# First-layer products of the experts: 512 moving columns in one product, or in two of 256

## The chip, the core and the metric

The kernel runs on one core of a Trainium2 chip. The metric is the device time of one execution in microseconds. Engines: PE is TensorE (PEld its loads of stationary operands), DVE VectorE, ACT ScalarE, POOL GpSimd, SP the queue that issues most DMAs.

## The reference

A recurrent attention (768 steps; 4 batches, 8 heads, a 40x40 state each) gives 3072 tokens of 320 numbers. A gate chooses two of eight experts for each token, and each expert is a two-layer network of 320 -> 1024 -> 320. Only the second part is touched:

```python
for e in range(E):
    for k in range(2):
        mask = top2[:, k] == e
        h = np.maximum(x[mask] @ w1[e], 0.0)
        out[mask] += top2_w[mask, k, None] * (h @ w2[e])
```

## The kernel before

The attention comes first, for some 600 us, in chunks of 64 steps; beside it the gate is worked out and tokens get slots in the experts' lists. Then the eight experts run one after the other. Each has room for 832 tokens, in two parts of 512 and 320 (`PARTS`).

For one expert, `load1` and `load2` fetch its float32 weights, and `loadx` gathers its tokens by indirect DMAs on POOL. `trans` (L268) turns the tokens round on PE, 128 at a time, into the PSUM tile `pt`. Weights and tokens are then split into a high and a low piece of type float32r (`split1`, `split2`, and the copies in `trans`), so that the products of pieces together keep float32's accuracy. ACT makes the high piece (w2h, L243) and DVE the low one (w2l, L244).

`hidden` is the first layer. For each part and each of eight blocks of 128 hidden units it takes a PSUM tile `ph` of 128x512 float32 (three buffers) and adds up eight products in it (L287): high by high, low by high, high by low, over 320 inputs in three slices. The moving operand is the tokens, so a product of part 0 has 512 moving columns and one of part 1 has 320. ACT then writes the rectified high piece `hh` (L288), and DVE subtracts for the low piece `hl` (L290), which frees the `ph` buffer.

`output` is the second layer: for each 128 tokens a PSUM tile `po` (three buffers) gets 24 products (L309), eight each of hh by w2h, hl by w2h and hh by w2l, all of 320 moving columns. The last 64 tokens go another way (L300, L301), and ACT (yl, L303) and DVE (y, L304) end them; for the others ACT alone writes y (L310). POOL adds y to the result by an indirect DMA (L311).

The order on each engine is set by the tile framework: it runs a timeline of its own over the program as written and places each instruction when it thinks its inputs are there. So first-layer products of an expert, second-layer products of the same one and transposes for the next stand mixed on PE. A product of float32r loads its own stationary operand: in the program it is one instruction, in the trace a load and a product.

Of the kernel before, what the change touches and what calls it, by code (L numbers as in the profile page):

```python
# [39 lines left out]
class Moe:  # L40
# [236 lines left out]
    def hidden(s,W,X,part):  # L277
        nc=s.nc; wh,wl=W; xh,xl,x3,x3l=X
        t0,n=s.parts[part]; t0%=CAP; r=slice(t0,t0+n)
        m=n//128*128; z=n-m  # L280
        hh=s.hp.tile([128,8,n+z],F32R,name=f"hh{part}"); hl=s.hp.tile([128,8,m],F32R,name=f"hl{part}")
        for f in range(8):
            fs=slice(128*f,128*f+128)
            ph=s.ph.tile([128,512],F32,name="ph",bufs=3)
            mm=[(wh[:,0,fs],xh[:,0,r]),(wh[:,1,fs],xh[:,1,r]),(wh[:,2,fs],x3[:,r]),(wl[:,0,fs],xh[:,0,r]),(wl[:,1,fs],xh[:,1,r]),
                (wh[:,0,fs],xl[:,0,r]),(wh[:,1,fs],xl[:,1,r]),(wh[:,2,fs],x3l[:,r])]
            for i,(a,b) in enumerate(mm): nc.tensor.matmul(ph[:,:n],a,b,start=i==0,stop=i==7)  # L287
            nc.scalar.activation(hh[:,f,:n],ph[:,:n],AF.Relu)  # L288
            for o,c in ((hl[:,f],slice(0,m)),(hh[:,f,n:],slice(m,n))):
                if c.stop>c.start: nc.vector.scalar_tensor_tensor(o,ph[:,c],0.0,hh[:,f,c].bitcast(F32),op0=ALU.max,op1=ALU.subtract)  # L290
        return hh,hl
# [606 lines left out]
```

## Time and profile before

| | |
|---|---|
| median of 3 runs | 1039.44 us (1037.34 to 1044.21) |
| profiled execution | 1035.52 us |
| its span, first to last instruction | 1033.7 us |
| busy: PE / PEld / DVE / ACT / POOL | 814.5 / 712.2 / 554.3 / 391.0 / 321.1 us |
| granted PE clock, mean over the span | 0.904 |

Products overlap in the pipeline and their ends are modelled, so the pace is read from start to start of groups rather than from the length of one. The clock column of a stretch is the share of full speed that was granted. In the waits an arrow names what ended the wait.

### The profile page before, as it was taken

The page shows a single profiled execution, that of the slowest core. Times are in us where ns is not written, and L with a number is a line of the kernel's source. Part 1 is how long each engine was busy: PE and PEld are TensorE (multiplying, and loading weights), DVE is VectorE, ACT ScalarE, POOL GpSimd, SP SyncE. Part 2 cuts the span into 40 slices and gives each one's busy share as a digit, 9 for nine tenths or more (in the row PEclk, how much of TensorE's full clock was granted, in tenths as well). Part 3 has the DMA queues.
Part 4 walks back from the last instruction along what each step waited for, and adds up shares of the span by engine and source line. Part 5 has one row for each costly group of instructions (what it writes and reads, how often), then busy time and mean ns, then how long its engine had stood idle before and what let it go on. Part 6 is the DMA issues. An engine that isn't in the chain of part 4 may idle for free.

```text
span 1033.7 us, 27409 instructions
## 1 busy us (share of the span) xinstructions
PE 814.5 (79%) x11706; PEld 712.2 (69%) x11706; DVE 554.3 (54%) x1198; ACT 391.0 (38%) x820; POOL 321.1 (31%) x456
## 2 busy tenths in 40 slices
PE   0114558669857876998896789999999999999994
PEld 0113446557746755877775668898989898989994
DVE  9268667944757666338554762643434444443420
ACT  2203443334633542454443432543434444443420
POOL 5000000393077039209401005316060606060312
PEclk9999986558967976998997699999999999999997
DMA  4785896593784684473486403516161616161302
GB/s 121 183 231 127 214 266 151 146 239 102 163 247 156 139 209 112 116 173 121 127 256 203 126 8 73 163 24 167 28 154 43 159 37 157 38 148 49 36 8 37
DMA packets 127111, 135.89 MB, mean 131 GB/s; under 512 B 59248, under 2 KB 106804, under 8 KB 126900
## 3 DMA queue, kind: packets, MB, share of 16 engines
q1 hardware_dynamic: 116292, 114.90, 41.5%
q0 software_dynamic: 10688, 19.14, 9.7%
q8 instruction: 94, 1.54, 0.6%
q14 instruction: 37, 0.30, 0.1%
HBM read 96.25 MB, written 41.03 MB: 133 GB/s over the span
## 4 chain that ended last, share of the span: by engine, by line
PE 53%; DVE 21%; DMA 14%; issue 4%; ACT 4%; SPq 3%; POOL 0%; POOLq 0%; DVEq 0%; ACTq 0%
PE po L309 17%; PE ph L287 15%; DMA rawk<-in_fm_dram 6%; PE psc L470 4%; PE pY L470 3%; DMA d_ab<-pk 2%; PE pW L470 2%; PE pQ L470 2%; PE pt L268 2%; DVE X L571 2%; DVE Tt L570 2%; DVE w2l L244 1%; DVE pk L460 1%; PE pst L470 1%; DVE ohB L162 1%
## 5 line engine op out<-in xcount | busy, mean ns | idle before, releaser
L311 POOL DMA_INDIRECT out_dram<-y,oi x56 | 92.3, 1648 | 236.9 <-ACT y L310 212.1
L290 DVE SCALAR_TENSOR_TENSOR hl<-ph,hh 128x256 fp32r<-128x256 f32 (+1 forms) x128 | 70.1, 554 | 120.5 <-ACT hh L288 111.3
L288 ACT ACTIVATE hh<-ph 128x320 fp32r<-128x320 f32 (+1 forms) x128 | 64.7, 518 | 147.6 <-PE ph L287 141.5
L564 POOL TENSOR_TENSOR X<-X,tri 128x1024 f32<-128x1024 f32 x4 | 9.0, 2242 | 309.2 <-DVE ak L606 179.3
L309 PE MATMUL po<-w2h,hh 128*128 128x320 f32 x384 | 75.4, 314 | 5.0 <-DVE y L304 3.9
L470 PE MATMUL psc<-RV,uT 128*64 128x128 f32 x384 | 63.0, 317 | 17.0 <-DVE P L680 15.1
L571 POOL TENSOR_TENSOR X<-X,Tt 128x30 f32<-128x30 f32 (+14 forms) x120 | 72.2, 602 | 8.7
L570 POOL TENSOR_TENSOR Tt<-X 128x30 f32<-128x30 f32 (+14 forms) x120 | 70.1, 584 | 8.4
L309 PE MATMUL po<-w2h,hl 128*128 128x320 f32 x384 | 70.8, 311 | 0.0
L287 PE MATMUL ph<-xh,w1h 128*128 128x512 f32 (+1 forms) x256 | 69.7, 355 | 1.0 <-DVE hl L290 1.0
L470 PEld LDWEIGHTS psc<-RV,uT 128*64 128x64 f32 x384 | 50.0, 160 | 27.6 <-DVE P L680 16.5
L287 PE MATMUL ph<-xh,w1l 128*128 128x512 f32 (+1 forms) x256 | 68.9, 350 | 0.0
L287 PE MATMUL ph<-xl,w1h 128*128 128x512 f32 (+1 forms) x256 | 68.6, 349 | 0.0
L252 POOL DMA_INDIRECT xr<-xd,gi x56 | 53.7, 959 | 47.6 <-issue 14.3
L309 PEld LDWEIGHTS po<-w2h,hh 128*128 128x128 f32 x384 | 61.0, 188 | 9.9 <-issue 5.0
L309 PE MATMUL po<-w2l,hh 128*128 128x320 f32 x384 | 65.7, 309 | 0.0
L470 PE MATMUL pQ<-w,T 32*32 32x40 f32 x2304 | 46.7, 224 | 23.7 <-DMA T<-scr 23.1
L680 DVE TENSOR_TENSOR P<-psc,mk 128x512 f32<-128x512 f32 x48 | 32.9, 686 | 59.3 <-PE psc L470 59.1
L470 PEld LDWEIGHTS pQ<-w,T 32*32 32x32 f32 x2304 | 39.6, 128 | 36.3 <-issue 32.1
L470 PE MATMUL psc<-RV 128*64 128x128 f32 x384 | 63.1, 317 | 0.0
L309 PEld LDWEIGHTS po<-w2h,hl 128*128 128x128 f32 x384 | 59.8, 188 | 0.5
L309 PEld LDWEIGHTS po<-w2l,hh 128*128 128x128 f32 x384 | 58.6, 188 | 0.1
(312 smaller groups left out, 1883.7 us busy)
## 6 DMA issues: line engine op xcount, KB each, us to landing
w2r<-in_w_dram SPq DMA_DIRECT2D x8, 1280.0 KB
RV<-in_rv_dram SPq DMA_DIRECT2D x48, 192.0 KB
rawba<-in_fm_dram SPq DMA_DIRECT2D x24, 360.0 KB
d_ab<-pk SPq DMA_DIRECT2D x24, 360.0 KB
st_ab<-d_ab SPq DMA_DIRECT2D x36, 240.0 KB
w1r<-in_w_dram SPq DMA_DIRECT2D x8, 1024.0 KB
raww<-in_fm_dram SPq DMA_DIRECT2D x12, 365.6 KB
st_ab<-d_ab SPq DMA_DIRECT2D x24, 180.0 KB
```

Of the source, the lines that this page charges most:

```text
L162: nc.vector.tensor_tensor(B[:,j],D[:,j].rearrange("p k (o m)->p k o m",o=1).to_broadcast([128,2,4,64]),vl[:,j].rearrange("p k (f o)->p k f ...
L252: k=t//128; nc.gpsimd.indirect_dma_start(out=X[:p,k if s.cap==CAP else 0],out_offset=None,in_=s.xd[int(w is not s.early[0])],in_offset=OFF ...
L268: for t,p in tiles(t0,n): nc.tensor.transpose(pt[:,t-t0:t-t0+p],x[:p,t//128,f0:f0+128],s.idm[:p,:p])
L287: for i,(a,b) in enumerate(mm): nc.tensor.matmul(ph[:,:n],a,b,start=i==0,stop=i==7)
L288: nc.scalar.activation(hh[:,f,:n],ph[:,:n],AF.Relu)
L290: if c.stop>c.start: nc.vector.scalar_tensor_tensor(o,ph[:,c],0.0,hh[:,f,c].bitcast(F32),op0=ALU.max,op1=ALU.subtract)
L309: s.lm=nc.tensor.matmul(po[:p],h[:,f,r],w[:,f],start=k==0,stop=k==23); k+=1
L311: st=nc.gpsimd.indirect_dma_start(out=s.out_d,out_offset=OFFS(ap=idx[:p,e,ii:ii+1],axis=0),in_=y[:p],in_offset=None,compute_op=ALU.add)
L470: def mm(s,*a,**k): return lambda: s.nc.tensor.matmul(*a,**k)
L570: eng.tensor_tensor(t,Xt[:,j:j+1,j+1:].to_broadcast([128,j,m]),Xt[:,0:j,j:j+1].to_broadcast([128,j,m]),op=ALU.mult)
L571: s.tl=eng.tensor_tensor(Xt[:,0:j,j+1:],Xt[:,0:j,j+1:],t,op=ALU.add)
L680: nc.vector.tensor_tensor(m,pp.rearrange("p i j t->p (i j) t"),s.mk.to_broadcast([128,8,64]),op=ALU.mult)
```

## The change

Where a part has 512 tokens, each of the eight products is issued as two, over columns 0 to 255 and 256 to 511 of the same `ph` tile, with the same stationary operand. The two halves of one product follow each other. Only the very first of the sixteen has the start flag, only the last pair the stop flag. Part 1 (320 columns) and the second layer stay as they are.

```diff
-            for i,(a,b) in enumerate(mm): nc.tensor.matmul(ph[:,:n],a,b,start=i==0,stop=i==7)
+            cut=[slice(0,256),slice(256,n)] if n==512 else [slice(0,n)]
+            for i,(a,b) in enumerate(mm):
+                for q in cut: nc.tensor.matmul(ph[:,q],a,b[:,q],start=i+q.start==0,stop=i==7,skip_group_check=True)
```

The framework's timeline comes out otherwise with it, so the order on PE moves in the expert stage. The first place is the start of the fourth expert, where the third to the seventh read alike (x_ with a number is the third slice of the tokens, hh_ with a number the rectified tile of the expert). Before, from the last first-layer product of the third block:

```order
L287 MATMUL ph<-x3l,w1h 128x512
L268 MATMUL pt<-idm,xr 128x128 x8
L309 MATMUL po<-w2h,hh_10841 128x320 x6
L287 MATMUL ph<-xh,w1h 128x512 x2
L287 MATMUL ph<-x_10582,w1h 128x512
L287 MATMUL ph<-xh,w1l 128x512 x2
```

The same place now, where line numbers behind the change are two higher:

```order
L289 MATMUL ph<-x3l,w1h 128x256 x2
L268 MATMUL pt<-idm,xr 128x128 x8
L311 MATMUL po<-w2h,hh_11033 128x320 x2
L289 MATMUL ph<-xh,w1h 128x256 x4
L289 MATMUL ph<-x_10774,w1h 128x256 x2
L289 MATMUL ph<-xh,w1l 128x256 x4
```

Two second-layer products stand ahead of the fourth block instead of six. The second place is where the others come, in the same expert after the first block of part 1. Before:

```order
L309 MATMUL po<-w2h,hh_10841 128x320 x3
L287 MATMUL ph<-xh,w1h 128x320 x2
L287 MATMUL ph<-x_10582,w1h 128x320
L287 MATMUL ph<-xh,w1l 128x320 x2
L287 MATMUL ph<-xl,w1h 128x320 x2
L287 MATMUL ph<-x3l,w1h 128x320
L309 MATMUL po<-w2h,hh_10841 128x320 x3
```

And now:

```order
L289 MATMUL ph<-xh,w1h 128x320 x2
L289 MATMUL ph<-x_10774,w1h 128x320
L289 MATMUL ph<-xh,w1l 128x320 x2
L289 MATMUL ph<-xl,w1h 128x320 x2
L289 MATMUL ph<-x3l,w1h 128x320
L311 MATMUL po<-w2h,hh_11033 128x320 x9
```

Nine second-layer products stand together where there were three ahead of the block and three behind it. POOL and SP keep their orders; ACT and DVE change places of a few instructions next to each other.

## Rows read from the trace of the kernel before

**Rows 1.** The page: busy us (share of the span) and instructions.
```profile
PE 814.5 (79%) x11706; PEld 712.2 (69%) x11706; DVE 554.3 (54%) x1198; ACT 391.0 (38%) x820; POOL 321.1 (31%) x456
```

**Rows 2.** The page: the chain that ended last, shares by line.
```profile
PE po L309 17%; PE ph L287 15%; DMA rawk<-in_fm_dram 6%; PE psc L470 4%; PE pY L470 3%; DMA d_ab<-pk 2%; PE pW L470 2%; PE pQ L470 2%; PE pt L268 2%; DVE X L571 2%; DVE Tt L570 2%; DVE w2l L244 1%; DVE pk L460 1%; PE pst L470 1%; DVE ohB L162 1%
```

**Rows 3.** Stretches: us, busy by engine (instructions), granted clock, DMA share, GB/s.
```profile
core 0: us, PE busy (x) PEld busy (x) DVE busy (x) ACT busy (x) POOL busy (x), PEclk, DMA share, GB/s
764.00:816.00 52.00, 50.73 (x309) 46.77 (x308) 21.41 (x40) 20.91 (x38) 18.09 (x15) 1.00 0.39 97
972.00:1020.00 48.00, 47.90 (x291) 44.84 (x289) 13.46 (x29) 13.94 (x28) 11.23 (x8) 1.00 0.20 23
```

**Rows 4.** Chain of waits, pieces in order: start us, us, what.
```profile
777.32 1.83 PE ph L287 x8
...
785.89 1.17 PE ph L287 x8
...
972.41 5.50 PE ph L287 x24
```

**Rows 5.** Chain of waits at the first expert's start.
```profile
602.19 0.33 PE px L97 x3
...
609.87 0.70 DVE hl L290
...
610.61 2.14 PE ph L287 x8
```

**Rows 6.** Timeline at 620 us: start us, us, engine, line, work.
```profile
620.25 0.61 PE L165 MATMUL pn<-ohB,ohA 128*128 128x256 f16 x4
```

**Rows 7.** Line L165: duration in ns, least/median/most.
```profile
L165 PE MATMUL pn<-ohB,ohA x48: 269/273/421, 349.4 to 620.6; 128*128 128x256 f16 x48
```

**Rows 8.** Groups by line and shape, 660 to 1020 us: busy us, mean ns.
```profile
L309 PEld LDWEIGHTS po<-w2h,hh 128*128 128x128 f32 x336 | 53.5, 188 | 9.1 <-issue 5.0 <-ACT hh L288 1.5
...
L290 DVE SCALAR_TENSOR_TENSOR hl<-ph,hh 128x512 fp32r<-128x512 f32 x56 | 37.6, 686 | 55.1 <-ACT hh L288 49.8 <-issue 5.2
...
L288 ACT ACTIVATE hh<-ph 128x512 fp32r<-128x512 f32 x56 | 32.3, 599 | 73.2 <-PE ph L287 71.0 <-issue 2.1
...
L268 PEld LDWEIGHTS pt<-idm,xr 128*128 128x128 f32 x112 | 13.6, 140 | 1.5
```

**Rows 9.** Timeline of PE's loads in the last expert.
```profile
1006.69 1.21 PEld L309 LDWEIGHTS po<-w2h,hh 128*128 128x128 f32 x8
```

**Rows 10.** Timeline of PE at the fourth expert's start.
```profile
764.17 0.64 PE L287 MATMUL ph<-xh,w1h 128*128 128x512 f32 x2
...
769.69 1.03 PE L268 MATMUL pt<-idm,xr 128*128 128x128 f32 x8
770.86 0.56 PE L309 MATMUL po<-w2h,hh 128*128 128x320 f32 x2
772.55 0.82 PE L309 MATMUL po<-w2h,hh 128*128 128x320 f32 x4 [1.13 <-DVE y L304]
773.21 0.39 PE L287 MATMUL ph<-xh,w1h 128*128 128x512 f32 x1
```

**Rows 11.** Waits from 600 us: us in total, times, longest.
```profile
PE po L309 <- DVE y L304: 3.9, 5, 1.1
```

**Rows 12.** Timeline of ACT at the fourth expert's start.
```profile
764.46 2.62 ACT L243 ACTIVATE w2h<-w2r 128x640 fp32r<-128x640 f32 x4 [1.85 <-PE po L301]
768.74 0.53 ACT L303 ACTIVATE yl<-po,tab 64x320 f32<-64x320 f32 x1 [1.66 <-PE ph L287]
```

**Rows 13.** Timeline of DVE at the same place.
```profile
768.80 3.03 DVE L244 TENSOR_TENSOR w2l<-w2r,w2h 128x640 fp32r<-128x640 f32 x4 [9.88 <-issue]
771.86 0.54 DVE L304 SCALAR_TENSOR_TENSOR y<-po,tab,yl 64x320 f32<-64x320 f32 x1
772.33 1.87 DVE L290 SCALAR_TENSOR_TENSOR hl<-ph,hh 128x512 fp32r<-128x512 f32 x3
```

## The prediction

> **What bounds the kernel now.** I read the busy shares first, then the shares of the chain that ended last, then the busy time by stage, then the single rows of one expert's start. TensorE is the busiest engine, 814.5 us of a span of 1033.7 us [rows 1], and its two expert lines, the second layer's products (L309) and the first layer's (L287), are 17% and 15% of the chain [rows 2]. By stage it is plainer: in the 52 us of one middle expert TensorE shows 50.73 us busy against 21.41 us of VectorE and 20.91 us of ScalarE, and in the 48 us of the last expert 47.90, both at a granted clock of 1.00 [rows 3]. So in the expert stage, from about 602 to 1020 us, nearly every nanosecond that TensorE spends more on its products moves the end. The attention stage before it is untouched: the change leaves the order of every engine as it was up to the first expert's products.
>
> **What one product costs.** Busy durations of products overlap, so I count from group to group. Eight first-layer products of 512 columns take 1.83 us, 228.8 ns each; eight of 320 columns take 1.17 us, 146.3 ns each [rows 4]. [...] No row shows a product of this type with 256 columns. [...] I take 119.5 ns, since 320 columns is the nearest row of the same type: two halves are 239 ns where one whole was 228.8, so **10 ns more for each split product**. The bounds: from below 110 ns, the transposes, which load a 128x128 float32 stationary operand each and follow one another every 0.33/3 us [rows 5]; float16 products of 256 columns with their loads come at (0.61 - 0.273)/3 = 112 ns, 0.273 being the length of the last one [rows 6, 7]. From above 146 ns, the product of 320 columns, which is wider and so cannot be cheaper.
>
> **The loads.** Each half issues its own load of the stationary operand, so 512 loads are added. A load lasts 188 ns on the record [rows 8], longer than the 146 ns between two products of 320 columns; eight loads there take 1.21 us in all, so one starts every (1.21 - 0.19)/7 = 146 ns and they overlap each other and the products [rows 9]. The load therefore needs at most 146 ns of its own, and the transposes (110 ns) say it needs about 110, just under the 119.5 of a half. [...]
>
> **How many of them count.** Eight experts have 8 blocks of 8 such products: 512 become 1024.
> - First expert: its first 24 wait for VectorE's routing work, which ends with the subtraction at 609.87 us, and the products start again at 610.61 after an idle stretch [rows 5]; these 24 hide. 40 count.
> - Second and last expert: all 64 each (the last starts with 24 in 5.50 us and goes on without a wait [rows 4]).
> - Third to seventh expert: the first 24 of each run into a wait that is there already. Products start at 764.17, the transposes of the next inputs at 769.69, two second-layer products at 770.86, and then TensorE stands 1.13 us until 772.55 for the output y of the expert before [rows 10]. That wait occurs five times, 3.9 us in all [rows 11]. What sets its end is elsewhere: ScalarE splits the second weights from 764.46, takes the last output at 768.74, VectorE splits from 768.80, writes y at 771.86 and subtracts at 772.33 [rows 12, 13]. So 24 hide and 40 count in each, 200 in all.
>
> 40 + 128 + 200 = 368 products at 10 ns: **3.7 us**.
>
> **What moves.** In these five starts the order puts two second-layer products ahead of the fourth first-layer block, where there were six. The third was the one that stood for y, so that wait goes; but the fourth block needs the buffer that VectorE's first subtraction frees, next in its queue: 772.33 + 0.686 = 773.02 us [rows 8, 13]. TensorE would be there at 764.17 + 48 x 0.1195 + 1.17 (transposes and the step behind them) + 2 x 0.146 = 771.37, and now stands 1.65 us. The block starts at 773.02 instead of 773.21 [rows 10], 0.19 us earlier, with four products of 146 ns, 0.59 us, still to do. Net +0.4 us in each, five times: **2.0 us**. The later regrouping (one product, then nine, where there were twos, threes and fours) finds its inputs ready, as the rectifier and subtraction of a block, 599 and 686 ns [rows 8], are shorter than a block. DMA queues and GpSimd keep their order; POOL waits for outputs, not the reverse.
>
> **Sum:** 3.7 + 2.0 = 5.7, say 6 us. The profiled execution took 1035.52 us (span 1033.7), so 1041.5 us for one like it. It lies 3.9 us under the median of the runs shown, 1039.44; against that median the forecast is **1045 us**, +0.6%. About 1% (10.4 us) is what a measurement here can tell from no change.
>
> **The rivals.**
> - **The load becomes the bound (slower).** If the load of this type needs more than 119.5 ns, a half comes at the load's pace. It decides from (228.8 + (10.4 - 2.0)/368 us)/2 = 126 ns, past which the whole is over 1%. At 130 ns it is 368 x 31 ns + 2.0 = +13 us, 1053; at the upper bound of 146 ns 368 x 63 ns + 2.0 = +25 us, 1065. For it: 188 ns on the record against 140 for the transposes' loads [rows 8]. Against: 110 ns in the transposes and no trace of it at 320 columns. Chance 0.20.
> - **The late signal comes sooner (no change).** ScalarE takes the last output at 768.74, though the next expert's products start at 764.17 [rows 10, 12]: the signal comes over 4 us late, after some 20 of those products, and I do not see why. If it hangs on their number and not on time, halves bring it 20 x (228.8 - 119.5) ns = 2.2 us earlier; the subtraction is then done before TensorE arrives at 771.37, and the fourth block starts 1.8 us sooner than before. Each of the five starts gains 1.8 - 0.6 = 1.2 us instead of losing 0.4: 3.7 - 6.0, about -2 us, 1037. Chance 0.14.
> - **The load is not repeated.** Two halves share a stationary operand; if the second load vanished, only the 2.0 us would be left, 1041.5. The order lists no loads for this type, so it cannot tell. Chance 0.04.
> - [...] Chance 0.02.
> - Both the late signal sooner and halves near 110 ns: 368 x (220 - 228.8) ns = -3.2, with the -6.0 above -9 us, 1030, and with noise over 1% faster. Chance 0.04.
>
> **Numbers.** Forecast 0.56; its own spread, a few microseconds between runs (1037.34 to 1044.21), puts a tenth of it over 1%. Range 1035 to 1056: the low end is the late-signal rival less noise, the high end the load rival to 132 ns; the load rival's rest, the bare loads and the fastest case stay out. Slower by over 1%: 0.20 + 0.02 + 0.05 less a little for a mild load bound, 0.25; faster 0.04; within 1% 0.71.
>
> **What will show it.** Sixteen halves should take 1.91 us where eight wholes took 1.83; a group of 2.1 us or more is the load rival, 1.83 the vanished load. The wait for y at the five starts should be gone, replaced by a wait of the fourth block for the subtraction of about 1.6 us; if ScalarE's last output moves from 4.6 us behind the first product to nearer 2.4, the late-signal rival holds. [...]

## The result, and the profile after

Twenty runs of each, in turn: 1048.87 us (1040.81 to 1058.97) against 1038.9 (1033.1 to 1046.13), ratio **1.0087**, 95% interval 1.0064 to 1.0111, so 9.0 us slower (6.6 to 11.5). The ratio leaves out the two longest runs of the change (1057.99 and 1058.97 us), which were in a slow state of the chip, so 9.0 is less than the 10.0 us between the medians. The forecast was 1045, 5.7 us slower. The profiled execution took 1050.84 us, span 1049.1; the first expert's products start in it 5.3 us later than in the profile of before (607.77 against 602.49), ahead of anything that the change moves, so the two profiles are compared expert by expert.

The page's first part, beside [rows 1]: 512 more products and 512 more loads, 9.3 us more of TensorE.

```profile
PE 823.8 (79%) x12218; PEld 743.8 (71%) x12218; DVE 553.7 (53%) x1198; ACT 392.6 (37%) x820; POOL 322.7 (31%) x456
```

Time of each expert in us, from the start of one expert's last second-layer product to that of the next (the first from its first product, the last to the end of the span):

| | 1 | 2 | 3 | 4 | 5 | 6 | 7 | 8 |
|---|---|---|---|---|---|---|---|---|
| before | 58.00 | 51.88 | 51.66 | 52.39 | 51.64 | 51.65 | 52.38 | 61.63 |
| after | 58.45 | 56.36 | 52.64 | 52.61 | 52.74 | 52.76 | 53.32 | 62.48 |
| more | 0.45 | **4.48** | 0.98 | 0.22 | 1.10 | 1.11 | 0.94 | 0.85 |

The sum is 10.1 us, and nearly half of it is one expert, the second. Its start, in the timeline of TensorE of the changed kernel:

```profile
673.08 0.40 PE L289 MATMUL ph<-x3l,w1h 128*128 128x256 f32 x2
673.32 0.60 PE L311 MATMUL po<-w2h,hh 128*128 128x320 f32 x3
676.15 0.45 PE L268 MATMUL pt<-idm,xr 128*128 128x128 f32 x1 [2.23 <-DMA xr<-xd,gi]
676.25 1.15 PE L311 MATMUL po<-w2h,hh 128*128 128x320 f32 x3
```

A transpose of gathered rows waits 2.23 us for its gather, and whatever is behind it in TensorE's order waits too. In the kernel before the first transposes of these rows stand behind six first-layer blocks and wait for nothing:

```profile
673.94 0.39 PE L287 MATMUL ph<-x3l,w1h 128*128 128x512 f32 x1
674.17 0.60 PE L268 MATMUL pt<-idm,xr 128*128 128x128 f32 x4
```

That is 13.7 us behind the expert's start at 660.49; in the changed order they stand behind three blocks and three second-layer products, 7.6 us behind it, and the gathers (669.24 to 678.13 us) are under way. The wait has a second price. Stretches around it, columns as in [rows 3]:

```profile
666.00:674.00 8.00, 7.92 (x61) 7.16 (x59) 6.23 (x10) 5.64 (x11) 5.77 (x6) 1.00 1.06 305
674.00:676.10 2.10, 0.00 (x0) 0.00 (x0) 0.69 (x1) 0.27 (x1) 1.49 (x3) 0.97 1.05 388
676.10:678.00 1.90, 1.85 (x8) 1.84 (x9) 0.00 (x0) 0.00 (x0) 1.59 (x2) 0.50 0.90 297
678.00:679.40 1.40, 1.40 (x9) 1.40 (x8) 0.00 (x0) 0.00 (x0) 1.09 (x2) 0.51 0.36 132
679.40:681.00 1.60, 1.60 (x15) 1.60 (x15) 0.00 (x0) 0.05 (x1) 0.52 (x1) 1.00 0.37 43
```

TensorE did nothing for 2.1 us, and the granted clock then stands at 0.50 for 3.3 us, in which it starts 17 products; at the 120 to 147 ns that they take at a clock of 1.00 it would be some 25, by estimate. Of the eight experts this one alone has a clock below 1.00, 0.97 in the mean (again 0.97 in the fourth series); before, all eight have 1.00. The gathers are slow to land here: the first starts at 669.24 and its transpose at 676.15, 6.9 us later, where the median gather lands after 2.9 us (fourth series). The DMA share of 1.05 goes with that, since the next expert's weights (w2r, issued at 669.75) are fetched at the same time. The kernel before has the slow landing too (6.5 us in the profile of the fourth series), but its transposes come later.

At the fourth expert's start, which [rows 10] show before, the wait for y is gone, and TensorE stands elsewhere:

```profile
775.37 0.66 PE L289 MATMUL ph<-xh,w1h 128*128 128x256 f32 x4
...
778.01 0.64 PE L289 MATMUL ph<-xh,w1l 128*128 128x256 f32 x4
778.50 1.00 PE L289 MATMUL ph<-xl,w1h 128*128 128x256 f32 x4
...
779.83 0.28 PE L289 MATMUL ph<-xh,w1h 128*128 128x256 f32 x1
780.55 0.60 PE L289 MATMUL ph<-xh,w1h 128*128 128x256 f32 x3 [0.44 <-issue]
...
782.42 1.03 PE L268 MATMUL pt<-idm,xr 128*128 128x128 f32 x8
783.21 0.54 PE L311 MATMUL po<-w2h,hh 128*128 128x320 f32 x2
783.59 0.64 PE L289 MATMUL ph<-xh,w1h 128*128 128x256 f32 x4
```

The halves run at 120 ns each (2.64 us for 22 of them, 775.37 to 778.01), as forecast. Then the stream breaks, with gaps of 0.26, 0.25 and 0.60 us between 778.7 and 780.6, and the profile shows nothing that TensorE waits for there ("issue"). The fourth block follows the second-layer products at 783.59 without a wait. ScalarE at the same place, beside [rows 12]:

```profile
776.28 2.62 ACT L243 ACTIVATE w2h<-w2r 128x640 fp32r<-128x640 f32 x4 [2.32 <-PE po L303]
779.15 0.53 ACT L305 ACTIVATE yl<-po,tab 64x320 f32<-64x320 f32 x1 [0.25 <-remote]
```

The last output is taken 3.8 us behind the first product (before: 4.6); "remote" says that the profile does not tell what ended the wait. Waits from 600 us on, beside [rows 11]: the row of y is no longer there.

```profile
PE ph L289 <- issue: 4.2, 8, 0.9
PE pt L268 <- DMA xr<-xd,gi: 2.8, 2, 2.2
```

So two things were open: what breaks the stream in five starts, and whether the order alone explains the second.

### The profile page after: what moved, and what is told of

It is laid out like the page before. It is cut to its first block, busy times and chain, and to the rows that moved or that the text cites. A ratio compares the mean times of both kernels' runs of the same rounds, so it can differ in the third digit from the quotient of the medians.

```text
span 1049.1 us, 28430 instructions
## 1 busy us (share of the span) xinstructions
PE 823.8 (79%) x12218; PEld 743.8 (71%) x12218; DVE 553.7 (53%) x1198; ACT 392.6 (37%) x820; POOL 322.7 (31%) x456
## 4 chain that ended last, share of the span: by engine, by line
PE 54%; DVE 16%; DMA 14%; issue 4%; POOL 4%; SPq 3%; ACT 3%; POOLq 0%; DVEq 0%; ACTq 0%
PE ph L289 18%; PE po L311 16%; DMA rawk<-in_fm_dram 5%; PE psc L472 3%; PE pY L472 3%; DMA d_ab<-pk 2%; PE pt L268 2%; DMA X<-scr 2%; PE pW L472 2%; PE pQ L472 2%; POOL X L573 2%; DVE X L573 2%; DVE Tt L572 2%; POOL Tt L572 1%; DVE pk L462 1%
## 5 line engine op out<-in xcount | busy, mean ns | idle before, releaser
L289 PE MATMUL ph<-xh,w1h 128*128 128x256 f32 (+1 forms) x384 | 71.6, 296 | 3.5 <-issue 2.2
L289 PE MATMUL ph<-xl,w1h 128*128 128x256 f32 (+1 forms) x384 | 71.6, 293 | 0.8 <-issue 0.6
L311 PE MATMUL po<-w2h,hh 128*128 128x320 f32 x384 | 71.5, 314 | 0.6 <-ACT hh L290 0.6
L289 PE MATMUL ph<-xh,w1l 128*128 128x256 f32 (+1 forms) x384 | 70.6, 293 | 0.0
L311 PE MATMUL po<-w2h,hl 128*128 128x320 f32 x384 | 68.6, 311 | 0.0
L289 PEld LDWEIGHTS ph<-xh,w1h 128*128 128x128 f32 x384 | 57.2, 191 | 6.4 <-issue 4.4
L244 DVE TENSOR_TENSOR w2l<-w2r,w2h 128x640 fp32r<-128x640 f32 x32 | 24.6, 821 | 66.5 <-ACT w2h L243 34.1
```

The lines of the kernel that those rows point to most:

```text
L244: nc.vector.tensor_tensor(l[:,k:k+2],w[:,k:k+2],h[:,k:k+2].bitcast(F32),op=ALU.subtract)
L289: for q in cut: nc.tensor.matmul(ph[:,q],a,b[:,q],start=i+q.start==0,stop=i==7,skip_group_check=True)
L311: s.lm=nc.tensor.matmul(po[:p],h[:,f,r],w[:,f],start=k==0,stop=k==23); k+=1
```

## The experiments

They ran in three series behind the first, which is that of the result; each shares its runs of before. Times of all experts, in us, are in a table at the end of this section. Of each edit only the lines that matter are shown.

**Second series: where the two costs sit.** A signal is the semaphore update by which a finished product releases what waits for it; it is called late where it comes more than half a microsecond behind the product's end. Theory A: 13 ns for each split product in all experts (0.83 us in an expert); stalls of about 1.2 us at five starts where TensorE's signals come late while GpSimd gathers, in place of the wait for y; and the second start.

`early_whole` and `early_halves`: before, and the change, with gathers moved away from the starts.

```
- name="xr")                                     + name="xr",bufs=2)
- r1=s.load1(e+1); xn=s.loadx(e+1); s.loadx(e+1,xn,1); r2=s.load2(e+1)
+ r1=s.load1(e+1)
+ with (s.tc.issue_after(s.adds[max(e-2,0)][-1].ins) if e else ExitStack()):
+     xn=s.loadx(e+1); s.loadx(e+1,xn,1)
+ r2=s.load2(e+1)
```

> The kernel before with a second buffer for the gathered rows xr, so that GpSimd's seven gathers for the next expert can run some 30 us earlier, in the first third of the expert ahead; TensorE's order from the third expert on is that of before. Theory A (while the gathers run, the signals of TensorE's finished products come 3.6 to 4.4 us late; the wait for y at five starts comes from that): at the third to seventh start ScalarE takes its last output within 1 us of the product's end, the waits of 0.6 to 1.3 us for y are gone, about 5 us faster than before, 1034; late signals turn up where the gathers now are. Rival B (the late signal belongs to the last products of an expert or to the scatters, not to the gathers): late signals stay where they were and the time is that of before, 1039.

> The changed kernel with the same second buffer and earlier gathers. Theory A (a half costs 120 ns, 13 ns more for each split product, 0.83 us in an expert, in all experts; beyond that the change costs stalls of about 1.2 us in the third to seventh start, where late signals keep finished products in TensorE's queue until it runs dry, and 2.4 to 3.6 us at the second start, where transposes now stand ahead of their gathers): both kinds of stall go, the product price of 6.7 us stays, so 6 to 7 us slower than the other kernel of this pair (before with earlier gathers) and 1 to 2 us slower than before, 1040 to 1041. Rival C (the stream of halves runs dry by itself, since its instructions can't be issued at that pace): the stalls at the starts stay, about 1046.

Measured: ratios 1.0103 (1.0059 to 1.0146) and 1.0215 (1.0167 to 1.0262). Both forecasts of the time missed. In the first two experts, where the edit puts 10 and 14 gathers in a row, `early_whole` takes 12.2 us more than before and `early_halves` 11.4 more than the change; how much of that the rows of gathers cost by themselves is not shown. What the edit did in the other experts is as theory A said: with whole products each takes 50.62 us, nothing waits, and ScalarE takes its last output 1.7 us behind the first product (776.37). So rival B falls, and with the clean starts of `early_halves` rival C. The weights' transfers (at the fourth expert's start from 763.05 and 779.68 us on) and the scatters stayed at the starts, so they alone don't make signals late.

```profile
775.39 2.62 ACT L243 ACTIVATE w2h<-w2r 128x640 fp32r<-128x640 f32 x4 [0.59 <-PE po L300]
778.04 0.53 ACT L303 ACTIVATE yl<-po,tab 64x320 f32<-64x320 f32 x1
```

The late signals went with the gathers, into the middle of the third to sixth expert of `early_halves`. In the third, with a set of seven gathers at 732.26 to 740.80, the signal of a product that ends at 739.23 comes 2.9 us late, and TensorE then stands 0.5 us for the subtraction that hangs on it; the three others read alike. And where ten gathers run in a row in `early_whole`, TensorE's timeline is broken up product by product:

```profile
635.62 0.90 PE L309 MATMUL po<-w2h,hl 128*128 128x320 f32 x5
636.87 0.31 PE L309 MATMUL po<-w2h,hl 128*128 128x320 f32 x1 [0.35 <-issue]
637.57 0.31 PE L309 MATMUL po<-w2h,hl 128*128 128x320 f32 x1 [0.39 <-issue]
638.27 0.30 PE L309 MATMUL po<-w2h,hl 128*128 128x320 f32 x1 [0.39 <-issue]
```

`halves_5of8` and `halves_3of8`: the two parts of the change alone.

```
- cut=[slice(0,256),slice(256,n)] if n==512 else [slice(0,n)]
+ cut=[slice(0,256),slice(256,n)] if n==512 and f>2 else [slice(0,n)]     (5of8; f<3: 3of8)
```

> The change without the first three blocks of each expert: only blocks four to eight are cut into halves, 320 of 512 products. Theory A: 320 x 13 ns = 4.2 us for the products; the first three blocks hold 48 queue entries for 5.5 us as before, so no stall inside them; the wait for y is back at five starts with the length that it had before; at the second start the transposes stand behind six blocks and wait for nothing: 4 to 5 us slower than before, 1043. Rival D (all of the 9 us are the price of the halves, 17.6 ns for each split product): 5.6 us slower with the same idle time as before.

> The other part of the change alone: only the first three blocks of each expert are cut into halves, 192 of 512 products. Theory A: 192 x 13 ns = 2.5 us for the products, stalls of about 1.2 us inside the third to seventh start in place of the wait for y (net within 0.3 us each), and the 2.4 to 3.6 us at the second start, where the transposes stand right behind three blocks as in the change: 5 to 6 us slower than before, 1044 to 1045. Rival D (the price of the halves alone): 192 x 17.6 ns = 3.4 us slower. Rival E (the stall hangs on the number of halves in an expert, not on the first blocks): no stalls at the starts, 2.5 us slower.

Measured: 1.0065 (1.0032 to 1.0097) and 1.0088 (1.0054 to 1.0122), 6.7 and 9.1 us, each a little over what was expected. With the first three blocks halved, the second expert has its wait for the gathers (56.03 us), and the starts have the broken stream; here the fourth expert's, after 32 halves, in the third block:

```profile
771.63 0.40 PE L289 MATMUL ph<-x3l,w1h 128*128 128x256 f32 x2
772.47 1.09 PE L289 MATMUL ph<-xh,w1h 128*128 128x256 f32 x4 [0.43 <-issue]
773.89 0.36 PE L289 MATMUL ph<-x,w1h 128*128 128x256 f32 x1 [0.34 <-issue]
```

With the first three blocks whole, the wait for y is back at four of the five starts (not at the third expert's), and nothing breaks there; the fourth expert's:

```profile
766.92 1.03 PE L268 MATMUL pt<-idm,xr 128*128 128x128 f32 x8
767.71 0.54 PE L311 MATMUL po<-w2h,hh 128*128 128x320 f32 x2
769.58 0.38 PE L311 MATMUL po<-w2h,hh 128*128 128x320 f32 x1 [1.33 <-DVE y L306]
```

One more expectation failed: the second expert of `halves_5of8` loses 2.1 us too, without a wait for gathers. A signal there is 4.0 us late, the halved blocks run on, and 30 products later TensorE stops, at 671.24, until the signal comes at 671.93. Rival D (only the price of the halves) falls: its 3.4 us for `halves_3of8` lie outside the interval (5.6 to 12.6 us), and beside the first profile of before the eight experts take 7.0 us more with 192 split products, 3.1 with 320. Rival E falls with the stalls at the starts.

**Third series: the cures.** `late_t_whole` keeps products whole, spreads the early gathers and holds the transposes of the first two experts; `halves_hold` is the change with one line of order put back; `plain_halves` does without gathers; `quarters` prices the load.

```
late_t_whole, halves_hold (the latter for e==1 alone, and without the lines of the gathers):
- W1=s.split1(r1); X=s.trans(xn); s.trans(xn,X,1)
+ W1=s.split1(r1)
+ with (s.tc.issue_after((s.hm[1][3] if e==0 else s.hm[0][5]).ins) if e<2 else ExitStack()):
+     X=s.trans(xn); s.trans(xn,X,1)
late_t_whole: xr bufs=2; for e==0, behind the output of part 0
+ with s.tc.issue_after(s.adds[0][3].ins): xn=s.loadx(1); s.loadx(1,xn,1)
and for e>0
+ g=s.adds[0][5] if e==1 else s.adds[1][0] if e==2 else s.adds[e-2][-1]
+ with s.tc.issue_after(g.ins): xn=s.loadx(e+1); s.loadx(e+1,xn,1)
plain_halves:
+ if e and s.cap==CAP: nc.sync.dma_start(X[:p,k],s.xd[1][128*k:128*k+p])      (else the gather as before)
quarters:
+ cut=[slice(128*j,128*j+128) for j in range(4)] if n==512 else [slice(0,n)]
```

> The kernel before, whole products, with two buffers for the gathered rows; for the third and later experts GpSimd's gathers are queued in the middle of the expert ahead and never two sets in a row, and in the first two experts TensorE's transposes of these rows are held behind the products that they stood behind before. Theory A (late signals go with the gathers; a set of seven in the middle of an expert is covered by whole products): the first two experts as in before, the third to seventh start without a wait for y, 50.6 us for each of these experts instead of 51.6 to 52.4, in all 6 to 7 us faster than before, 1028 beside 1034. Rival B (what the first run with earlier gathers lost in its first two experts, 12 us, is a lasting price of gathers beside products): no faster than before.

> The changed kernel, with one thing undone: at the second expert's start TensorE's transposes of gathered rows are held behind the sixth first-layer block, about where they stood before. Theory A: the wait of 2.2 us for the gathers at that place goes, and what follows it there; the second expert takes 52.7 to 53.5 us instead of 56.4, the other experts as in the change, so 5.5 to 6.5 us slower than before instead of 9. Rival F (TensorE is held there by late signals and would stand as long behind any other work): the second expert still takes 55 to 56 us, 9 us slower than before.

> The changed kernel, with the gathers for the second to eighth expert replaced by plain transfers of as many rows in their stored order, queued by SP; the experts then work on other rows, and GpSimd has only the scatters left. TensorE's order from the second start on is that of the change but for the transposes. Theory A: it is GpSimd's gathers that hold back TensorE's signals, so signals come within 0.3 us, the stalls inside the third to seventh start are gone, these experts take 51.4 us instead of 52.6 to 53.3, and the second 52 to 53; about 1 us faster to 1 us slower than before. Rival G (any transfer into these rows, or the scatters, or the weights' transfers hold the signals back): stalls of about 1.2 us stay in each start, 5 us slower or more.

> The changed kernel with four products of 128 columns in place of two of 256: 2048 products and as many loads. It measures how near the load is to being the bound. If a product costs 0.43 ns per column and 10 to 13 ns besides, with the load hidden, quarters come every 65 to 68 ns. If the load needs the 109 to 110 ns of the transposes, they come every 110 ns, each of the 512 wholes then takes 440 ns instead of 227, and the expert stage takes some 109 us longer. Theory A says the second, which leaves 10 ns of cover at 256 columns; with the rival (no bound by loads at all) it is about 20 us longer.

Measured: `late_t_whole` 0.997 (0.9936 to 1.0003), no faster; `halves_hold` 1.0062 (1.0028 to 1.0097), 6.4 us slower, as expected; `plain_halves` 1.0009 (0.9975 to 1.0043), as expected; `quarters` 1138.94 us in its one run, 107 over before.

`halves_hold` settles the second start: held behind the sixth block, the transpose waits for nothing, the granted clock stays at 1.00, and the expert takes 52.51 us, 4 us less than with the changed order (56.36, and 56.60 in the fourth series); no other expert's order on TensorE differs from the change's. The times by themselves, 6.4 us over before against 8.5 and 9.0, are too near for their intervals to tell that. Rival F falls with the fourth series, where the wait stands without any late signal.

```profile
673.72 0.40 PE L290 MATMUL ph<-x3l,w1h 128*128 128x256 f32 x2
673.96 0.27 PE L268 MATMUL pt<-idm,xr 128*128 128x128 f32 x1
673.98 0.72 PE L290 MATMUL ph<-xh,w1h 128*128 128x256 f32 x4
```

`quarters` settles the load: eight quarters start every 0.89 to 0.90 us, 111.5 ns each (the median over 2048), and not 67.

```profile
740.15 1.06 PE L289 MATMUL ph<-xh,w1l 128*128 128x128 f32 x8
741.05 1.06 PE L289 MATMUL ph<-xl,w1h 128*128 128x128 f32 x8
741.94 0.61 PE L289 MATMUL ph<-x3l,w1h 128*128 128x128 f32 x4
```

But one thing in this series was expected by nobody: the third to seventh expert of `halves_hold` take 51.33 us each, where TensorE's order is the same as in the change (52.6 to 53.3). No signal is late in any of the four profiles, with gathers or without: from the first expert on each comes within 25 ns of its product's end, even in the first expert, where the program is the same as in profiles that had late ones. So `plain_halves` and `late_t_whole` told nothing of the cause.

**Fourth series: the control.** The change and before once more, as they are, beside two kernels of the third.

> The changed kernel once more, as it is. All four profiles of the last job showed no late signal at all, with gathers or without, in places where the program is the same as in earlier profiles that had them; so lateness may belong to the chip that a job gets. Theory A2 (on some chips the signals of finished products come late while GpSimd's gathers run, on others never; the second start's wait for the gathers is a matter of order and comes on every chip): where this job's signals are late, the third to seventh expert take 52.6 to 53.3 us each, otherwise 51.3 us; the second expert takes over 55 us in either case; about 9 us slower than before in either case, since before loses its waits for y too. Rival H (the kernel decides whether signals are late): late signals as in the first profile of this kernel, whatever the other three show.

> The kernel before, once more, for a profile on the same chip as the other three. Theory A2: with late signals 51.6 to 52.4 us for the third to seventh expert and waits for y of 0.6 to 1.3 us; without them 50.6 us for each and no wait for y. Rival H: waits for y as in its first profile.

> Whole products with the earlier gathers and the transposes held, as in the last job. Theory A2: where this job's signals are late, 50.6 us for the third to seventh expert instead of 51.6 to 52.4, 6 us faster than before; where they are prompt, nothing to gain, within 2 us of before.

> The changed kernel with plain transfers of rows in their stored order in place of the gathers for the second to eighth expert, as in the last job. If this job's signals are late in the other kernels, theory A2 expects none late here and 51.3 us for the third to seventh expert; rival G (transfers, scatters or weights hold the signals back, not the gathers) expects stalls of about 1.2 us at each start. If the signals are prompt in the others too, this run tells nothing between them but the price of the second start's wait: 52.5 us for the second expert here, over 55 in the changed kernel.

Measured: 1.0082 (1.0056 to 1.0109) for the change, 0.9993 (0.9966 to 1.0019) for `again_late_t`, 1.0036 (1.001 to 1.0061) for `again_plain`, and one run of before with a span of 1027.8. No signal was late here either, so rival H falls: the kernel doesn't decide it. Before, without late signals, fourth expert's start; the wait for y of [rows 10] is not there:

```profile
769.28 1.03 PE L268 MATMUL pt<-idm,xr 128*128 128x128 f32 x8
770.07 1.13 PE L309 MATMUL po<-w2h,hh 128*128 128x320 f32 x6
771.03 0.63 PE L287 MATMUL ph<-xh,w1h 128*128 128x512 f32 x2
```

The change at the same start; 48 halves from 775.47 to 781.24, 120 ns each, and no break:

```profile
775.47 0.66 PE L289 MATMUL ph<-xh,w1h 128*128 128x256 f32 x4
...
781.24 1.03 PE L268 MATMUL pt<-idm,xr 128*128 128x128 f32 x8
782.03 0.54 PE L311 MATMUL po<-w2h,hh 128*128 128x320 f32 x2
782.41 0.64 PE L289 MATMUL ph<-xh,w1h 128*128 128x256 f32 x4
```

The wait at the second start is there as in the first profile, and it is the only one left from 655 us on:

```profile
PE pt L268 <- DMA xr<-xd,gi: 2.4, 1, 2.4
```

| | late signals | 1 | 2 | 3 to 7 | 8 |
|---|---|---|---|---|---|
| early_whole | yes | 64.48 | 57.61 | 50.62 each | 61.9 |
| early_halves | yes | 63.75 | 62.43 | 51.94, 51.91, 51.92, 51.93, 51.33 | 62.5 |
| halves_5of8 | yes | 58.36 | 54.01 | 51.08, 52.64, 51.93, 51.97, 51.93 | 62.4 |
| halves_3of8 | yes | 58.06 | 56.03 | 52.34, 52.51, 52.31, 52.42, 52.37 | 62.2 |
| late_t_whole | no | 58.70 | 51.88 | 50.62 each | 61.8 |
| halves_hold | no | 58.42 | 52.51 | 51.33 each | 62.6 |
| plain_halves | no | 58.06 | 52.51 | 51.33 each | 61.3 |
| again_before | no | 57.87 | 51.88 | 50.62 each | 61.7 |
| again_change | no | 58.37 | 56.60 | 51.33 each | 62.4 |

The two others of the fourth series repeat theirs within 0.2 us. No version beats the kernel before by more than its interval.

## Why the prediction was right, and where it was wrong

- **The price of a half.** Forecast 119.5 ns, measured 120 (the median over 1024). No run shows the 119.5 itself, the author's estimate: before, no product of this type has 256 columns, and the line through its two widths, (228.8 - 146.3)/192 = 0.43 ns per column, gives 146.3 - 64 x 0.43 = 118.8 by estimate. Forecast 10 ns more for each split product, measured (51.33 - 50.62) us / 64 = 11, from the fourth series. Right; theory A's 13 was too much.
- **The loads are hidden.** Right, with little to spare: quarters, with half the columns, come no faster than every 111.5 ns, so halves have 8.5 ns of cover. The forecast took 110 from the transposes. The rival of the load as the bound falls. Loads overlap running products here: at 320 columns the spacing stays 147 ns with loads of 188 ns [rows 8].
- **First and last expert.** Forecast 0.4 and 0.64 us, measured 0.45 to 0.50 and 0.63 to 0.85. Right.
- **Second expert, "all 64", 0.64 us.** This is the step that failed: the forecast counted the products there and put the new order at nothing. The expert costs 4.5 us more (4.7 in the fourth series), in both cases some 4 over the forecast. It read the order of the third to seventh expert, where work "finds its inputs ready" if the rectifier and the subtraction are done, and never asked for the rows that GpSimd gathers, though in the second expert TensorE's transposes of them had moved from behind six blocks to behind three. Putting them back takes 4 us off. The wait is 2.2 to 2.4 us of it; most of the rest goes with the half clock behind it, by the estimate above.
- **Third to seventh expert, 0.8 us each.** The sum, 4.35 us for the five against 4.0, is right by luck, since the way was another. The wait for y went, as said; the wait of 1.65 us of the fourth block for the subtraction did not come (at the seventh start alone there is one, of 0.3 us). In its place the stream of halves stood for 1.3 to 1.5 us. That stop and the lost wait for y nearly cancel: beside the periods of the fourth series the late signals cost the five experts 6.6 us before the change and 7.4 with it. And all 64 products count at 11 ns, not 40: the fourth series shows 0.71 us in each of these experts with neither of the two waits.
- **The late signal comes sooner with more products.** The rival fell: the last output is taken 3.8 us behind the first product instead of 4.6, not 2.4, and where signals are prompt it is 1.7 us in both kernels (765.44 behind 763.77, 777.15 behind 775.47).

By the terms: 10.1 us in the first pair of profiles and 0.50 + 4.72 + 5 x 0.71 + 0.6 = 9.4 in the pair of the fourth series, against 5.7; what is missing is the second start, some 4 us. The forecast of 5.7 us lies 3.3 under the measured 9.0, inside its range.

## What to carry to other kernels

When a planner orders the work, a finer grain also moves what stands between the pieces: go through every instruction that changed its place, and ask for each what it reads and when that lands, transfers by another engine above all. Halving moving columns costs about 11 ns a product here, where a half at 120 ns is still longer than the 111.5 ns at which quarters came, each with its load; those cost 107 us. A wait that a profile shows at five places can belong to that execution alone: a second profile of the same kernel had none.

## What the runs showed that was not expected

**Where signals were late, the stream of halves broke some 30 products behind the one whose signal was out.** In six profiles signals of finished products came late, mostly by 1 to 5 us, and with two exceptions (0.6 and 2.2 us) only from 1 us ahead of a set of gathers to 6 us behind its last. Whole products run on through it: 17 to 20 of them fit into 3.7 to 4.4 us [rows 10, 12]. Halves don't: in the change the first gap comes 27 to 29 products behind the last one of the expert before, whose signal is 3.6 to 4.3 us late, and the long one behind 31 to 33; in `halves_3of8` the first comes behind 31 to 33, in `halves_5of8`, in the second expert, behind 30. Theory A put the break down to a queue of TensorE that held products fill, and counted 48 entries for three whole blocks, a load and a product each (24 of each are in the trace). That was the author's estimate: no record shows such a queue or its entries, and it would not explain all of the gaps. The long gap of the change begins 0.1 to 0.8 us after that last signal has come, at the fourth expert's start at 779.95 behind 779.12, when the next product whose signal is out, the last of the first block, is only 15 to 17 products back; and in `halves_3of8` the last signal of the third to sixth expert was in 0.8 to 1.0 us before the first gap. What is measured is that TensorE goes on beside a held signal twice: at 779.12 with the first, at 780.55 0.11 us ahead of the next (780.66). Why the long gap starts where it does stays open.

**Whether signals are late is not the kernel's doing.** All six profiles of the first two series had it and all eight of the last two had none, the change and before among both; the second and the fourth series ran on a chip of the same number. That it goes with GpSimd's gathers where it occurs is shown by moving them within the second series. The six profiles also hold fewer records: 12312 to 12537 semaphore updates against 13307 to 13325 in the eight, and of those that tell how GpSimd's own transfers land 38 to 47% are missing. Whether the recording itself holds signals back is a rival that no run here tests. What decides between the two, and by what path gathers hold a signal back, stays open; a run without gathers beside a control with late signals would tell, and the two tries met prompt signals. The ratio hardly depends on it: 1.0087 in the first series, 1.0082 in the fourth.
